# Feed-forward rows of the last quarter stored from V's buffer instead of the Q/K buffer, and one Wo load of segment 0 issued behind a flush

## The chip, the cores and the metric

The kernel runs on one core of a Trainium2 chip. The metric is device time in microseconds (us), the median of several executions; smaller is better. Five engines work side by side, each on its own queue of instructions, and wait for each other by semaphores: PE (matmuls and transposes), ACT, DVE, POOL and SP. SP does no arithmetic; it issues DMAs, and so do POOL and, in a few places, ACT. A wait holds up everything that stands behind it on the same queue.

## The reference

Two blocks work on the same `x` (2048 rows of 1024) and are mixed row by row with a gate. Block A is attention in segments of 32 rows: each segment sees its own rows and 8 memory rows that the segment before it left behind, so the segments run one after the other. Block B is a feed-forward block. All inputs are bf16.

```python
def _A_ref(x, mem0, Wq, Wk, Wv, Wo, seg_len):      # 32 heads of 128, M = 8, seg_len = 32
    ...
    for s in range(n_seg):                          # 64 segments
        xs = x[:, s * seg_len:(s + 1) * seg_len, :].copy()
        h = jnp.concatenate([mem, xs], axis=1)
        q = jnp.einsum('btd,dhe->bhte', h, Wq)
        k = jnp.einsum('btd,dhe->bhte', h, Wk)
        v = jnp.einsum('btd,dhe->bhte', h, Wv)
        scores = jnp.einsum('bhqe,bhke->bhqk', q, k) * scale
        scores = jnp.where(mask[None, None], scores, -1000000000.0)
        p = _softmax(scores, axis=-1)
        o = jnp.einsum('bhqk,bhke->bhqe', p, v)
        o = jnp.einsum('bhte,hed->btd', o, Wo)
        mem = o[:, :M, :].copy()
        outs.append(o[:, M:, :])
    return jnp.concatenate(outs, axis=1)

def _B_ref(x, w_gate, w_up, w_down):                # 3584 hidden columns
    return _gelu(x @ w_gate) * (x @ w_up) @ w_down

g = _sigmoid((x * gate_w).sum(-1, keepdims=True))
return g * a + (1 - g) * b
```

## The kernel before

**The order of the work.** First the feed-forward block runs over four quarters of 512 rows. Its results, already multiplied by 1 - g, go to `b_scr` in device memory. Then the 64 segments of block A run one by one; each adds its rows of `b_scr` at its end and stores 32 output rows. There is no planner: the order of instructions in the program text is the order on each engine's queue. A small scheduler (`_Sched`) keeps, for each named key such as `("qk", 0)`, who wrote it and who reads it. An instruction that writes a key waits for all earlier readers and writers of it, an instruction that reads a key for its writers. A DMA counts as a reader until it has landed.

**Where the weights are.** Wq, Wk, Wv and Wo don't fit on the chip beside the rest. Some of their 128-row pieces stay in `arena` for the whole run. The others are streamed in every segment through `ring`, ten places of 1024 columns, filled two at a time from a packed copy `w_scr` (line 624, on SP's queue). A load for the ring is issued when PE has read the piece that held the places.

**The end of the feed-forward block.** The last quarter is finished by `down_out` (line 499), called twice. It takes four results of 128 rows out of PSUM into four buffers: ACT takes the left halves (line 510), DVE the right halves (line 514). Each buffer is then stored to `b_scr` in five pieces (line 519). The list `bout` names the buffers and their keys: entries 0 and 1 are ring places, entry 2 is the buffer `qk`, entry 3 the buffer `oe`; `last_bout` holds two more, and the last quarter uses these two and entries 2 and 3. The pieces of entries 2 and 3 are issued on ACT's queue behind all others, those of the other buffers on POOL's. The DMA of an entry reads the entry's keys, so whoever writes the buffer next waits for its landing.

**Segment 0.** It is written out by hand (lines 1194 to 1273), as it does more than the others: it also computes q, k and v for the memory rows of the first four segments (`emit_ext`, line 862) and sets some streamed weight pieces aside (`keep`: PE transposes on line 931, a copy by DVE on line 937). The names used below:

- `emit_P` (line 980): the projections q, k, v from the rows `hT`; when a q or k projection is done, ACT copies it to `rows` (line 986).
- `emit_T`: transposes `rows` on PE (line 1019) and copies the result to `qk`, on DVE (line 1027) or on ACT (line 1025). `emit_T(0)` in segment 0 is the first writer of `qk` after the feed-forward block.
- `end_ext` (line 880) copies a finished projection of memory rows to a staging piece of the arena's chunk 20. For q and k it queues a pair (`go`, `put`): transposes on PE (line 894), four copies by DVE (line 907) and a store to `qk_scr` on POOL (line 910). `flush()` and `first_go()` issue what is queued.
- For v the staging piece is stored to `v_scr` on POOL (line 883), and `load_vte` (line 727) takes the memory rows of V from it into `vt`.
- `emit_vt` (line 1011): ACT copies V from PSUM to `vt`.
- `load_o3(k, xs)` (line 921): a load on POOL of 256 KB of Wo into quarter `k` of chunk 20, the same memory that holds the staging pieces `xs`, so it waits until those have been read. Segment 0 has four of them. Quarter 2 lies over the staging of v of the first half of the heads, quarter 1 over that of k.
- `emit_S`, `emit_PT`, `emit_PV`: scores with softmax, transposes of the probabilities, and the product with V.
- `emit_O` (line 1142): the output projection. Its last round in segment 0, `emit_O(3, ALL)`, takes the Wo pieces in the order 3, 4, 5, 6, 7, 2, 0, 1; pieces 0 to 3 are the quarters of chunk 20.

The last lines of `POOL`'s queue in segment 0 come in this order: the loads of `vt`, the store of `v_scr`, `load_o3(0, ..)`, `load_o3(2, ..)`, the store of `qk_scr` that `flush()` issues, `load_ext` (line 718), `load_x` (line 412), `load_o3(1, ..)`, a second store of `v_scr`, `load_xe` (line 418) and `load_b` (line 744).

Of the kernel before, what the change touches and what calls it, by code (L numbers as in the profile page):

```python
# [26 lines left out]
class _Sched:  # L27
# [10 lines left out]
    def op(self, eng, mk, r=(), w=(), dsem=None):  # L38
        o = _Op(eng, mk, dsem)
        deps = []  # L40
        if eng == "pool" and dsem is None:
            w = [*w, ("pool",)]
        for k in r:
            deps += self.w.get(k, ())
            if k[0] == "P":
                deps += [x for x in self.r.get(k, ()) if x.eng != eng]
        for k in w:
            deps += self.w.get(k, ())
            deps += self.r.get(k, ())
        for k in r:  # L50
            self.r.setdefault(k, []).append(o)
        for k in w:
            self.w[k] = [o]
            self.r[k] = []
        seen = set()
        for d in deps:
            if d is o or id(d) in seen:
                continue
            seen.add(id(d))
            if d.eng == eng and d.dsem is None and (eng == "pe" or eng == "sp"):  # L60
                continue
            o.deps.append(d)
            d.sig = True
        self.ops.append(o)
        return o
# [63 lines left out]
def bass_gated_mix__memory_aug_recurrent_mem_tr__geglu_ffn__prompt_kernel(  # L129
# [38 lines left out]
    with ExitStack() as es:  # L168
# [14 lines left out]
        def SB(shape, dt, name):  # L183
            return es.enter_context(nc.sbuf_tensor(name, list(shape), dt))
# [6 lines left out]
        qk = SB([128, 2, 4, L, 4], BF16, "qk")  # L191
        qkst = SB([128, 2, 4, EXT * 4], BF16, "qkst")
        vt = SB([128, 2, 512], BF16, "vt")
# [25 lines left out]
        def P(i):  # L219
            return ("P", i)  # L220
# [15 lines left out]
        def chunk(c):  # L236
            return arena[:, c * (CH // 2):min((c + 1) * (CH // 2), 21 * (CH // 2) + 2048)]
# [197 lines left out]
        def emit_H(b, j):  # L435
# [31 lines left out]
            if j % 4 == 3:  # L467
# [1 line left out]
                next_slab()  # L469

        bout = [(ring[:, RING - 2 + i, :], [("ring", RING - 2 + i, hf) for hf in range(2)]) for i in range(2)]
        bout += [(qk[:, :, :, :, :].rearrange("p a b c d -> p (a b c d)")[:, 0:1024], [("qk", 0), ("qk", 1), ("qke",)]),
                 (oe[:, :, :].rearrange("p a b -> p (a b)"), [("oe", x) for x in range(NO)])]

        last_bout = [(extra[:, :], [A(23)]), (arena[:, 21 * (CH // 2) + 1024:21 * (CH // 2) + 2048], [A(22)])]
# [111 lines left out]
        def uses(s, m, h, k):  # L587
            if m == "o":
                return 0 if k < 4 or (m, h, k) in single else (1 if (h, k) == (3, 5) else 2 * (k % 2))
            if m == "q" and h == 0 and s == 0 and k in (4, 5):  # L590
                return k - 3
            return 2 if k >= 6 and not (s and (m, h, k) == ("k", 0, 6)) else 0
# [36 lines left out]
        def slot_free(k):  # L629
            free[0] += k  # L630
            while n_str[0] < len(stream) and free[0] >= 2:
                free[0] -= 2
                stream_next()
# [78 lines left out]
        def acc(s, use):  # L712
            return (7 * s + USES[use]) % 2
# [41 lines left out]
        def unit(s, m, o, k):  # L755
            h = o // 2
            if m == "o":
                if (m, o, k) in single:
                    ap, key = single[(m, o, k)]
                    return [ap[:, 0:512], ap[:, 512:1024]], [key]  # L760
                if k >= 4:
                    sl = slot_of[(s, (m, 3, 5), 0)] if (o, k) == (3, 5) else slot_of[(s, (m, o, k - k % 2), k % 2)]
                else:
                    c, x = place[("o", o)], k
                    if o == 3:
                        y = k * 1024
                        return [chunk(c)[:, y:y + 512], chunk(c)[:, y + 512:y + 1024]], [("A20", k)]
            else:
                j = o % 2
                if (m, o, k) in single:  # L770
                    ap, key = single[(m, o, k)]
                    return [ap[:, 0:512], ap[:, 512:1024]], [key]
                if (m, h, k, j) in BACK:
                    if s > 0:
                        return BACK[(m, h, k, j)]
                    sl = slot_of[(s, (m, h, k), j if k >= 5 else 0)]
                elif k >= 6:
                    sl = slot_of[(s, (m, h, k), j)]
                elif m == "v":
                    c, x = place[("v", k)], o  # L780
                else:
                    c, x = place[(m, h, k // 2)], (k % 2) * 2 + j
            if uses(s, m, o if m == "o" else h, k) or (m == "o" and k >= 4):
                return [ring[:, sl, 0:512], ring[:, sl, 512:1024]], [("ring", sl, 0), ("ring", sl, 1)]
            return [chunk(c)[:, x * 1024 + 512 * y:x * 1024 + 512 * (y + 1)] for y in range(2)], [A(c)]
# [22 lines left out]
        def resident(m, h, kc):  # L808
            return not uses(1, m, h, kc) and not any((m, h, kc, j) in BACK for j in range(2))
# [7 lines left out]
        for s in range(NSEG):  # L817
# [20 lines left out]
            def begin(y):  # L838
                while y in order and order[0] != y:
                    later.pop(0)()  # L840
# [4 lines left out]
            def flush():  # L845
                while post:
                    go, put = post.pop(0)
                    put(go())
# [71 lines left out]
            def load_o3(k, xs):  # L920
                op("pool", lambda e: e.dma_start(chunk(20)[:, k * 1024:(k + 1) * 1024], A_Wo[24 + k, :, :]),
                   w=[("A20", k)] + [("rx", x) for x in xs], dsem=("b1", "b2", "b3", "a20")[k])
# [48 lines left out]
            def emit_P(m, h, pos, s=s):  # L971
                bank = acc(s, (m, h))
                for x in pos:
                    kc = KORD[(m, h)][x] if s else KCS.get((m, h), KCS[0])[x]
                    us = [unit(s, m, 2 * h + j, kc) for j in range(2)]

                    def mk(e, us=us, kc=kc, x=x):
                        ins = None
                        for gq in range(4):
                            ins = e.matmul(PB[bank][32 * gq:32 * gq + 32, :], lhsT=hT[:, kc, :],  # L980
                                           rhs=us[gq // 2][0][gq % 2],
                                           start=(x == 0), stop=(x == KC - 1), skip_group_check=True)
                        return ins
                    op("pe", mk, r=[("hT",)] + us[0][1] + us[1][1], w=[P(bank)])
                    if pos[-1] == KC - 1 and x == KC - 1 and m != "v":
                        op("act", lambda e: e.activation(rows[:, :], PB[bank][:, :], ACTF.Copy), r=[P(bank)], w=[("rows",)])  # L986
                    for _ in range(1 + len(kept) % 2):
                        if kept and (m, h) != ("q", 0):
                            kept.pop(0)()
                    if (m, h) in jobs and not (order and resident(m, h, kc)):  # L990
                        begin((m, h))
                        lag.append((us, kc))
                    elif (m, h) not in jobs or s:
                        slot_free(uses(s, m, h, kc))
                    if s or (m, h) == ("q", 0) or x >= 4:
                        while lag:
                            us, kc = lag.pop(0)
                            emit_ext(m, h, us + [kc])
                            held = [j for j in range(2) if s == 0 and (m, h, kc, j) in KEPT]
                            for j in held:  # L1000
                                keep(us[j], KEPT[(m, h, kc, j)], 5 if m == "q" else acc(0, ("q", 1)), 2 if j == held[-1] else 0)
                            if not held:
                                slot_free(uses(s, m, h, kc))
                    if (m, h) == ("q", 0):
                        for _ in range(1 + len(kept) % 2):
                            if kept:
                                kept.pop(0)()
# [186 lines left out]
            if s == 0:  # L1194
# [34 lines left out]
                emit_S(1)  # L1229
                emit_qke(1, ms=(0,))  # L1230
                load_o3(0, (0, 1))
                load_o3(2, (4,))
                emit_T(0, "act")
                emit_P("k", 1, (4, 5, 6, 7))
                emit_P("v", 1, (0, 1, 2))
                emit_T(1)
                emit_P("v", 1, (3,))
                flush()
                emit_P("v", 1, (4,))
                emit_PV(0)  # L1240
                emit_PT(1)
# [242 lines left out]
```

## Time and profile before

Three executions took 2459.4, 2468.72 and 2475.57 us. The profiled one took 2465.32 us.

| | before |
|---|---|
| median of the runs | 2468.72 us (2459.4 to 2475.57) |
| profiled execution | 2465.32 us |
| its span, first to last instruction | 2463.5 us |
| PE, DVE, ACT, POOL busy, share of the span | 90%, 47%, 39%, 26% |
| mean granted PE clock | 0.987 |
| moved by DMA | 781.03 MB, mean 317 GB/s |
| last quarter's feed-forward results leave PSUM | 597.9 to 600.7 us |
| segment 0 ends, segment 1 begins | about 655 us |

The profile is one execution. Each instruction has a start and a length; an engine's idle time before an instruction is put down to the semaphore that came last. Three things help in reading it. A wait can have several causes at once, and only the last one is named, so that the time that one cause costs is counted from the moment when all the others are over. The granted clock of PE is 1.00 or lower; at 0.50 matmuls take twice as long. And DMA share is the mean busy share of the core's 16 DMA engines: at 1.00 no more can be moved at a time.

### The profile page before, as it was taken

The numbers are of one execution on the slowest core, as the hardware profiler recorded it, in microseconds if no ns is written. First come the engines' busy times: TensorE is split into PE (matmuls) and PEld (weight loads), VectorE is DVE, ScalarE is ACT, GpSimd is POOL, SyncE is SP. The second block draws the span as 40 slices with busy tenths as digits, with TensorE's granted clock in tenths as the row PEclk, the third lists the DMA queues.
The fourth block names the chain that finished last, engine by engine and source line by source line (L and its number), as shares of the span: only waits on it lengthen the run. The fifth ranks groups of instructions, "written<-read, shape, count | busy, mean of one in ns | idle before, by whom it ended". The sixth has DMA issues, their size and how long they took to land.

```text
span 2463.5 us, 84811 instructions
## 1 busy us (share of the span) xinstructions
PE 2215.3 (90%) x37643; PEld 1117.8 (45%) x37699; DVE 1152.6 (47%) x3259; ACT 959.0 (39%) x2275; POOL 628.7 (26%) x1122
## 2 busy tenths in 40 slices
PE   8999999999888888988888888888888888988887
PEld 4444444444444444444444444444444444444444
DVE  5626264350444444454544444444444444444444
ACT  4314132230344444444444444444444444444443
POOL 1010102200323233232323332323323232323322
PEclk9999999999899999999999999999999999999989
DMA  8726354467899999999999999999999999999998
GB/s 263 273 69 236 118 181 128 120 214 286 304 343 363 358 363 339 363 374 358 373 368 363 363 367 364 368 370 367 359 356 361 369 371 362 371 365 361 377 372 302
DMA packets 294014, 781.03 MB, mean 317 GB/s; under 512 B 48305, under 2 KB 112993, under 8 KB 292881
## 3 DMA queue, kind: packets, MB, share of 16 engines
q1 hardware_dynamic: 240308, 703.76, 78.0%
q0 software_dynamic: 43072, 54.77, 7.3%
q10 hardware_dynamic: 10268, 17.08, 1.9%
q8 instruction: 297, 4.87, 0.8%
q14 instruction: 69, 0.56, 0.1%
HBM read 748.00 MB, written 37.22 MB: 319 GB/s over the span
## 4 chain that ended last, share of the span: by engine, by line
PE 59%; DMA 31%; DVE 5%; ACT 4%; issue 2%; POOL 0%; ACTq 0%; DVEq 0%; POOLq 0%
DMA ring<-w_scr 27%; PE pba L980 9%; PE pbb L980 9%; PE pbc L862 4%; PE pbe L1019 3%; ACT rows L986 2%; PE pba L449 2%; PE pbb L1142 2%; PE pbb L449 2%; PE pbg L449 2%; PE pbd L449 2%; PE pbf L449 2%; PE pbh L449 2%; PE pbc L449 2%; PE pbe L449 2%
## 5 line engine op out<-in xcount | busy, mean ns | idle before, releaser
L980 PE MATMUL pba<-arena,hT 128*32 128x512 bf16 x4416 | 370.9, 382 | 0.9 <-issue 0.9
L980 PE MATMUL pbb<-arena,hT 128*32 128x512 bf16 x4416 | 365.6, 383 | 0.1
L730 POOL DMA_DIRECT2D vt<-v_scr x252 | 147.1, 585 | 532.1 <-PE pbe L1100 210.2
L1094 DVE COPY ptb<-pbe 80x320 bf16<-80x320 bf16 x256 | 82.1, 321 | 317.3 <-PE pbe L1089 317.3
L862 PE MATMUL pbc<-arena,xe 128*32 128x512 bf16 x2208 | 203.9, 384 | 2.0 <-issue 1.4
L1027 DVE COPY qk<-pbe 128x512 bf16<-128x512 bf16 x129 | 89.1, 690 | 220.3 <-PE pbe L1019 211.3
L1072 ACT ACTIVATE pbd<-pbd 104x160 f32<-104x160 f32 x256 | 71.9, 281 | 299.2 <-DVE pbd L1070 299.2
L1438 POOL DMA_DIRECT2D out_dram<-bo x252 | 125.5, 505 | 201.2 <-DVE bo L1432 191.9
L980 PE MATMUL pbb<-ring,hT 128*32 128x512 bf16 x1412 | 136.4, 385 | 26.4 <-DMA ring<-w_scr 19.8
L980 PE MATMUL pba<-ring,hT 128*32 128x512 bf16 x1414 | 136.2, 383 | 26.4 <-DMA ring<-w_scr 21.3
L980 PEld LDWEIGHTS pba<-arena,hT 128*32 128x32 bf16 x4416 | 114.6, 97 | 82.2 <-issue 5.4
L980 PEld LDWEIGHTS pbb<-arena,hT 128*32 128x32 bf16 x4416 | 114.4, 97 | 79.6 <-issue 3.9
L986 ACT ACTIVATE rows<-pba 128x512 bf16<-128x512 f32 x128 | 76.4, 597 | 185.3 <-PE pba L980 183.3
L1079 DVE TENSOR_TENSOR pn<-pbd,rr 104x256 bf16<-104x256 f32 (+1 forms) x512 | 141.9, 318 | 8.7
L1142 PE MATMUL pbb<-ring,oT 128*32 128x256 bf16 x1792 | 103.7, 280 | 36.2 <-DMA ring<-w_scr 34.8
L1108 ACT ACTIVATE oT<-pbe 128x256 bf16<-128x256 f32 x256 | 97.2, 380 | 99.4 <-PE pbe L1100 97.9
L986 ACT ACTIVATE rows<-pbb 128x512 bf16<-128x512 f32 x128 | 76.4, 597 | 144.1 <-PE pbb L980 140.0
L1089 PE MATMUL pbe<-ident,pn 104*80 104x104 bf16 x1024 | 96.7, 217 | 37.3 <-DVE pn L1079 21.3
L1142 PE MATMUL pba<-ring,oT 128*32 128x256 bf16 x1792 | 102.9, 284 | 27.5 <-DMA ring<-w_scr 27.1
L1019 PE MATMUL pbe<-ident,rows 128*32 128x128 bf16 x4096 | 103.9, 221 | 26.2 <-ACT rows L986 12.5
L910 POOL DMA_DIRECT2D qk_scr<-rowsx x60 | 47.0, 783 | 308.2 <-DVE rowsx L907 306.2
L1073 DVE TENSOR_REDUCE rs<-pbd 104x4 f32<-104x160 f32 x256 | 83.0, 324 | 88.9 <-ACT pbd L1072 88.9
(268 smaller groups left out, 4529.9 us busy)
## 6 DMA issues: line engine op xcount, KB each, us to landing
ring<-w_scr SPq DMA_DIRECT2D x1153, 512.0 KB, 6.4
arena<-in_B_w_gate_dram SPq DMA_DIRECT2D x27, 1024.0 KB, 5.4
arena<-in_B_w_up_dram SPq DMA_DIRECT2D x27, 1024.0 KB, 7.6
qk<-in_A_Wq_dram ACTq DMA_DIRECT2D x63, 256.0 KB, 6.9
qkst<-qk_scr POOLq DMA_DIRECT2D x126, 64.0 KB, 5.4
qk_scr<-rowsx POOLq DMA_DIRECT2D x60, 128.0 KB, 5.6
arena<-in_B_w_down_dram SPq DMA_DIRECT2D x7, 1024.0 KB, 11.9
arena<-in_A_Wk_dram SPq DMA_DIRECT2D x6, 1024.0 KB, 6.5
```

The costliest lines, as they stand in the source:

```text
L449: ins = e.matmul(PB[bank][:, :], lhsT=wv[:, kc, col:col + 128], rhs=xb[:, kc, :], start=(kc == 0), stop=(kc == KC - 1))
L730: op("pool", lambda e: e.dma_start(vt[2 * SEG:KEYS, par, :], v_scr[s // GR, h, 2 * par:2 * par + 2, s % GR, :, :]), r=[("vscr", s // GR, h ...
L862: ins = e.matmul(PB[B_X][32 * gq:32 * gq + 32, :], lhsT=xe[:, us[-1], :], rhs=us[gq // 2][0][gq % 2], start=(n == 0), stop=(n == KC - 1), ...
L980: ins = e.matmul(PB[bank][32 * gq:32 * gq + 32, :], lhsT=hT[:, kc, :], rhs=us[gq // 2][0][gq % 2], start=(x == 0), stop=(x == KC - 1), ski ...
L986: op("act", lambda e: e.activation(rows[:, :], PB[bank][:, :], ACTF.Copy), r=[P(bank)], w=[("rows",)])
L1019: ins = e.transpose(PBV[B_T][j:j + 32, i * 128:(i + 1) * 128], rows[:, i * 128 + j:i * 128 + j + 32], ident[:, :])
L1027: op("dve", lambda e: e.tensor_copy(qk[:, m, :, 0:SEG, :], src), r=[P(B_T)], w=[("qk", m)])
L1079: op("dve", lambda e, c0=c0, k0=k0, n=n: e.tensor_tensor(out=pn[0:104, :, c0:c0 + 2 * n].rearrange("p i (two c) -> p i two c", two=2), in0 ...
L1089: ins = e.transpose(PBV[B_PT][0:KEYS, i * 128:i * 128 + 104], pn[0:104, i, :], ident[0:104, 0:104])
L1108: op("act", lambda e: e.activation(dst, src[:, :, :, 0:SEG], ACTF.Copy), r=[P(B_PV)], w=[("oT", o % 2)])
L1142: ins = e.matmul(PB[B_O][32 * q:32 * q + 32, 0:256], lhsT=oT[:, o % 2, k, :], rhs=u[q // 2][:, (q % 2) * 256:(q % 2 + 1) * 256], start=(o ...
L1438: op("sp" if last else "pool", lambda e, d=d, b=b: e.dma_start(d, b), r=[("bo", x)], w=[("out", s, x)], dsem="%s%d" % ("end" if last else ...
```

## The change

Two edits. In `bout`, entry 2 becomes the buffer `vt`, seen as 1024 columns, with the six keys `("vt", z)`, `("vte", z)` and `("vte", z, 0)`, in place of the first 1024 columns of `qk` with its three keys. Eviction, stores and queues stay as they are. In segment 0, `load_o3(2, (4,))` moves from behind `load_o3(0, (0, 1))` to behind `flush()`.

```diff
         bout = [(ring[:, RING - 2 + i, :], [("ring", RING - 2 + i, hf) for hf in range(2)]) for i in range(2)]
-        bout += [(qk[:, :, :, :, :].rearrange("p a b c d -> p (a b c d)")[:, 0:1024], [("qk", 0), ("qk", 1), ("qke",)]),
+        bout += [(vt[:, :, :].rearrange("p a b -> p (a b)"), [("vt", z) for z in range(2)] + [("vte", z) for z in range(2)] + [("vte", z, 0) for z in range(2)]),
                  (oe[:, :, :].rearrange("p a b -> p (a b)"), [("oe", x) for x in range(NO)])]
...
                 load_o3(0, (0, 1))
-                load_o3(2, (4,))
                 emit_T(0, "act")
                 emit_P("k", 1, (4, 5, 6, 7))
                 emit_P("v", 1, (0, 1, 2))
                 emit_T(1)
                 emit_P("v", 1, (3,))
                 flush()
+                load_o3(2, (4,))
                 emit_P("v", 1, (4,))
```

## The prediction

> **What bounds the kernel now.** I read the page's chain first, then the list of waits between 600 and 700 us, then the timelines around the two edited places, then the windows. By the chain, PE holds 59% of the span and DMA 31%, 27% of it ring<-w_scr. Two windows give the frame (columns of the windows: stretch, its length, busy us of PE, PEld, DVE, ACT and POOL, granted PE clock, DMA share, GB/s):
>
> ```profile
> 612.00:664.00 52.00, 41.59 (x796) 21.88 (x800) 20.22 (x67) 16.41 (x37) 15.39 (x27) 0.84 0.79 271
> 655.00:2463.00 1808.00, 1582.36 (x34076) 822.33 (x34068) 855.95 (x2790) 772.23 (x1866) 539.59 (x955) 0.99 0.99 361
> ```
>
> Three stages: feed-forward to about 600 us, segment 0 to about 655, then 63 segments of (2463.5 - 655) / 63 = 28.7 us, in which the DMA engines are full (0.99) and PE waits for the ring of weights. The diff touches only the seam between the first two stages and segment 0, where the DMA share is 0.79 and the clock 0.84: there time can go, and what goes there moves the whole tail forward unchanged. The waits there:
>
> ```profile
> DVE qk L1027 <- DMA b_scr<-qk: 9.0, 1, 9.0
> ...
> PE pbf L931 <- DVE arena L937: 4.9, 1, 4.9
> ```
>
> DVE waits 9.0 us for the store that reads qk, PE only 4.9 us behind DVE. Which of the two counts is read from the timeline (start, length, instruction, idle time before it and its releaser):
>
> ```profile
> 608.24 0.40 PE L1019 MATMUL pbe<-ident,rows 128*32 128x128 bf16 x16
> ...
> 608.78 0.62 PE L931 MATMUL pba<-ident,ring 128*128 128x128 bf16 x8
> ...
> 609.56 0.39 PE L980 MATMUL pbb<-ring,hT 128*32 128x512 bf16 x4
> 613.49 0.69 DVE L1027 COPY qk<-pbe 128x512 bf16<-128x512 bf16 x1 [8.97 <-DMA b_scr<-qk]
> 614.10 0.68 DVE L937 COPY arena<-pba 128x1024 bf16<-128x1024 bf16 x1
> 614.84 0.39 PE L931 MATMUL pbf<-ident,arena 128*128 128x128 bf16 x2 [4.89 <-DVE arena L937]
> ```
>
> The copy's own input, the transposes of line 1019, is complete at 608.24 + 0.40 = 608.64. Of DVE's 8.97 us only 613.49 - 608.64 = 4.85 are owed to the store.
>
> The second place is POOL's queue at the end of segment 0, and the PE instruction that waits at its end:
>
> ```profile
> 634.91 0.56 POOL L921 DMA_DIRECT2D arena<-in_A_Wo_dram  x1 [2.57 <-DVE qk L1027]
> 637.76 0.56 POOL L921 DMA_DIRECT2D arena<-in_A_Wo_dram  x1 [2.29 <-DMA v_scr<-arena]
> 638.39 0.76 POOL L910 DMA_DIRECT2D qk_scr<-arena  x1
> ...
> 644.09 0.54 POOL L921 DMA_DIRECT2D arena<-in_A_Wo_dram  x1 [3.60 <-DMA qk_scr<-arena]
> ...
> 649.62 0.65 PE L1142 MATMUL pba<-arena,oT 128*32 128x256 bf16 x8
> 652.05 0.41 PE L1142 MATMUL pba<-arena,oT 128*32 128x256 bf16 x4 [1.79 <-DMA arena<-in_A_Wo_dram]
> ```
>
> The second of these lines 921 is the load that is moved. It waits for the landing of v_scr's store (issued at 631.78, landed at 637.15), and the store of line 910 stands behind it on the queue; the third line 921 waits for that store's landing (643.80), lands at 644.09 + 7.92 = 652.01, and PE starts at 652.05.
>
> **The buffer, term A.** Nothing is added: the same evictions (lines 510 and 514, 0.7 us each) and the same five stores on ACT's queue, from vt. Without the wait the copy of line 1027 runs 608.69 to 609.38, the copy of line 937 follows its transposes (608.78 + 0.62 = 609.40) from 609.41 to 610.10, and PE starts line 931 at 610.15, not 614.84: 4.7 us. PE's last work before it ends at 609.95, so the gap shrinks from 4.89 to 0.2.
>
> The wait goes to V's first writers: ACT's copies of line 1011, seen at 629.0, and POOL's four loads of line 727, at 629.7. Moved forward by A and B they come at about 622.8, and the stores land at about 613.4, so the wait costs nothing with 9 us to spare. If that cover were gone, ACT would hold the softmax exponentials behind it and POOL the v_scr store. What is late next is the ring: v's second ring place is needed at 623.47 - 6.2 = 617.2. Its load is issued when the second group of line 931 frees a slot (616.80, so now about 611.4). The five ring loads from 616.80 to 626.17 took 3.7 to 6.5 us, those of 601 to 604, behind Wo and the stores, 9.1 to 9.7. The older transfers end by 612.2 (the DMA share falls to 0.17 in 612 to 613), so I take about 5 us and no wait; the other end, 9.7 us, is a wait of 3.9.
>
> **The clock, term B.** The stall throttles PE:
>
> ```profile
> 618.00:619.00 1.00, 1.00 (x13) 0.53 (x14) 0.00 (x0) 0.35 (x1) 0.00 (x0) 0.50 1.04 229
> ...
> 620.00:622.00 2.00, 2.00 (x68) 1.20 (x64) 1.06 (x5) 0.00 (x0) 0.38 (x1) 1.00 0.51 209
> ```
>
> The granted clock is 0.94 in 612 to 613, when PE has stood for 2 to 3 us, 0.50 until 619, and 1.00 from 620. From 614.84 to 619.4 PE works at clock 0.50. The eight transposes take 1.03 us there against 0.62 at 608.78, and four ext matmuls 0.62 against 0.40. Laid out at full speed, with the round trip over DVE kept (second group done at 611.32, DVE copy to 612.05, third group from 612.10, four matmuls), the ring matmuls seen at 618.99 start at 612.87, 6.12 us earlier; the transposes of line 894, which wait for ACT, come at 613.75, not 620.00. A and B together are 6.2, so B is 1.5. Its ends are 0, if a throttled window falls there all the same, and 2.2, the work halved.
>
> The Trainium skill ("TensorE: Matmul & The Clock Gate", Part 1) says that a free-running window of about 3.4 us decides, and that an idle one halves the clock. By that rule a gap of 0.2 us keeps the clock, the trace agrees for the 4.89 us gap, and A and B stand; read as a bound on single gaps it fails in the trace, where the clock is 0.50 at 650 after no PE gap over 2.0 us.
>
> **The Wo load, term C.** One POOL issue (0.56 us) moves behind flush(), past flush's store of line 910 on POOL; nothing of it crosses SP's queue. The store's data is there when DVE ends line 907 at 636.16. POOL is idle from 635.47, starts its DMAs 0.3 to 0.7 us after a release here, and issues at about 636.7, not 638.39. It lands after the same 5.41 us at 642.1, the last Wo load goes at 642.4, lands after 7.92 us at 650.3, and PE starts then instead of 652.05: 1.7 us. PE could take it from about 650.05, so at most 2.0. The loads of line 412, 418, 744 and 883 behind it come no later. The moved load, now at about 637.5 behind the store, lands after its 5.71 us at 643.2 for a use after 649: six us of cover; the slowest POOL transfer there (8.1 us) still fits. The last Wo load now shares DMA with the ring load of 640.39 that PE waits for at 646.45. Its 256 KB at the 361 GB/s of the tail are 0.7 us, so the cost is 0 to 0.7; I take 0, because it is issued 2 us after it. If the clock window of 647 to 657 (0.50) ends one step sooner, up to 1.7 us more are won; I take 0, since the 2.0 us ring wait that opens it stays.
>
> **Sum.** 4.7 + 1.5 + 1.7 = 7.9 us from span 2463.5: 2455.6. The profiled execution took 2465.32, 1.8 more than its span, so 2457.4. It lies 3.4 below the median of the runs shown, 2468.72; from that the forecast is 2461. The DMA engines can carry it: 612 to 664 moved 52 x 271 = 14.1 MB, 39 us at the tail's 361 GB/s, so 13 us are free.
>
> **Rivals.**
> *The ring is late.* The store traffic meets the earlier PE, v's second place comes at the 9.7 us of the loads of 601 to 604, PE waits 3.9, and the clock halves again for 1.5: 2.5 us gained, 2466. For it: DMA is at 0.99 to 1.05 until 612. Against: 5 us of empty DMA follow.
> *The bytes decide.* From 600 on, 64 x 285 and then 1799 us at 361 GB/s make 668 MB in 1863.5 us, 358 GB/s. If that is all the memory gives, nothing is won: 2469. Against: 397 GB/s in 608 to 610 and 375 in 850 to 900. The Trainium skill ("DMA: Bandwidth & Descriptors", Specifications) gives about 358 GB/s per core as the memory's limit, which is this rival exactly; the two windows above it speak against a hard limit.
> *The diff does more.* If DVE's whole 8.97 us were the store's, and the clock window at 647 closed, 4.1 + 1.7 more: 2455. The 608.64 above excludes the first half.
> *Slower.* In the tail a ring load that comes too late leaves PE idle, and a stretch at clock 0.50 follows, as from 804.0 to 807.4: 3.4 us at half speed, 1.7 us of PE. The three windows with clock 0.97 (800 to 850, 900 to 1000, 2000 to 2463) lose 0.03 x 613 = 18 us to them, some eleven such stretches. Where they fall depends on how loads and matmuls are phased, and the shift changes the phase. Five more outweigh 7.9 us; ten more give 2468.7 - 7.9 + 17 = 2478. For it: the three runs of one kernel span 16 us. Against: no edit touches a segment after the first, so such events are as likely to be fewer. For over 1%, twenty more are needed.
>
> **Chances.** Forecast 0.62, ring late 0.13, bytes 0.08, more 0.07, slower 0.10. About 1% (24.7 us) is what a measurement of this kernel tells from no change, the runs shown spreading 0.65%. All cases but extreme ones of the last two lie inside it: faster 0.04, same 0.93, slower 0.03. The range: the forecast's own terms run from 7.9 - 1.5 - 0.7 to 7.9 + 0.7 + 0.3 + 1.7, so 2458 to 2463; taking in the late ring and the bytes (2469) and half the 16 us spread of the runs at the lower end gives 2450 to 2470.
>
> **What would show it.** Right: DVE's line 1027 starts near 608.7 with a releaser on PE; no PE gap over 1 us before line 931 and the clock at 1.00 from 600 to 635; line 910 ahead of the second line 921 on POOL, about 5.4 us before the last Wo load; PE's last line 1142 at about 644; segment 1 some 8 us sooner. Wrong: a PE wait on ring<-w_scr near 617, ACT's line 1011 released by b_scr<-vt, or a tail longer than 1808 us.

## The result, and the profile after

The changed kernel takes 2456.09 us (median of 18 runs, 2448.88 to 2471.76), the kernel before, in the same sessions, 2465.99 us (18 runs, 2456.58 to 2475.57). The ratio is 0.9965, with a 95% interval of 0.9948 to 0.9982: 4.4 to 12.8 us less. The forecast was 7.9 us less.

The profiled execution has a span of 2447.1 us, 16.4 below the one of before. That is more than the medians say, and the marks of the two traces show where it comes from. From here on "the seam" is the time from the first eviction of the last quarter (ACT, line 510) to the transposes of line 1420 that end segment 0, and "the tail" what follows.

| | before | after | difference |
|---|---|---|---|
| start to first eviction | 597.93 | 595.79 | -2.14 |
| seam | 55.01 | 47.84 | -7.17 |
| tail | 1810.56 | 1803.44 | -7.12 |
| span | 2463.5 | 2447.1 | -16.4 |

Only the seam holds an edit; the other two rows come back below. The timeline of the changed kernel around the first edit (start, length, instruction, idle time before it and its releaser):

```profile
606.15 0.40 PE L1019 MATMUL pbe<-ident,rows 128*32 128x128 bf16 x16
606.37 0.39 PE L980 MATMUL pbb<-arena,hT 128*32 128x512 bf16 x4
606.60 0.69 DVE L1027 COPY qk<-pbe 128x512 bf16<-128x512 bf16 x1 [4.21 <-PE pbe L1019]
606.70 0.62 PE L931 MATMUL pba<-ident,ring 128*128 128x128 bf16 x8
607.25 0.40 PE L862 MATMUL pbc<-arena,xe 128*32 128x512 bf16 x4
607.35 0.69 DVE L937 COPY arena<-pba 128x1024 bf16<-128x1024 bf16 x1
607.47 0.39 PE L980 MATMUL pbb<-ring,hT 128*32 128x512 bf16 x4
608.10 0.56 PE L931 MATMUL pbf<-ident,arena 128*128 128x128 bf16 x7 [0.24 <-DVE arena L937]
```

DVE still sits idle for 4.21 us before its copy, now until PE's transposes are done: this part of the 8.97 us was never the store's. PE waits 0.24 us in place of 4.89. Windows (stretch, length, busy us of PE, PEld, DVE, ACT and POOL, granted clock, DMA share, GB/s) show the clock at 1.00 through the place where it fell to 0.50, and the DMA engines without the hole that stood there. The first line is from the kernel before, behind its stall, the other two from the changed kernel:

```profile
614.80:617.00 2.20, 2.16 (x20) 1.76 (x24) 0.24 (x1) 0.00 (x0) 0.00 (x0) 0.50 0.04 7
```

```profile
600.00:612.00 12.00, 11.04 (x204) 6.07 (x200) 3.47 (x6) 2.28 (x4) 2.70 (x5) 1.00 1.01 349
612.00:620.00 8.00, 7.52 (x178) 4.03 (x174) 5.42 (x23) 1.48 (x4) 3.16 (x5) 1.00 0.91 337
```

POOL's queue at the end of segment 0, changed kernel:

```profile
623.15 0.56 POOL L883 DMA_DIRECT2D v_scr<-arena  x1
626.24 0.56 POOL L921 DMA_DIRECT2D arena<-in_A_Wo_dram  x1 [2.52 <-DVE qk L1027]
627.98 0.76 POOL L910 DMA_DIRECT2D qk_scr<-arena  x1 [1.18 <-DVE arena L907]
628.98 0.54 POOL L921 DMA_DIRECT2D arena<-in_A_Wo_dram  x1 [0.24 <-issue]
...
635.50 0.54 POOL L921 DMA_DIRECT2D arena<-in_A_Wo_dram  x1 [3.64 <-DMA qk_scr<-arena]
```

The store of line 910 now goes ahead of the moved load. But the last Wo load comes 7.52 us after it, against 644.09 - 638.39 = 5.70 before. The view of the store alone gives its time from issue to landing, min, median and max, first before, then after:

```profile
DMA to landing us min/median/max: 5.4/5.4/5.4
```

```profile
DMA to landing us min/median/max: 7.2/7.2/7.2
```

In these two profiles the 1.8 us by which the store is issued sooner are lost before it lands. What still waits at the end of the seam, on PE, changed kernel:

```profile
637.56 0.61 PE L1142 MATMUL pba<-ring,oT 128*32 128x256 bf16 x8 [1.51 <-DMA ring<-w_scr]
...
642.74 0.40 PE L1142 MATMUL pba<-arena,oT 128*32 128x256 bf16 x4 [0.98 <-DMA arena<-in_A_Wo_dram]
```

### The profile page after: what moved, and what is told of

Read it like the earlier page. It is cut to its first block, busy times and chain, and to the rows that moved or that the text cites. A ratio compares the mean times of both kernels' runs of the same rounds, so it can differ in the third digit from the quotient of the medians.

```text
span 2447.1 us, 84869 instructions
## 1 busy us (share of the span) xinstructions
PE 2212.5 (90%) x37699; PEld 1115.9 (46%) x37699; DVE 1153.2 (47%) x3259; ACT 958.3 (39%) x2275; POOL 628.5 (26%) x1122
## 4 chain that ended last, share of the span: by engine, by line
PE 60%; DMA 30%; DVE 4%; ACT 4%; issue 2%; POOL 0%; SPq 0%; DVEq 0%; POOLq 0%
DMA ring<-w_scr 28%; PE pba L980 9%; PE pbb L980 9%; PE pbc L862 4%; PE pbe L1019 3%; ACT rows L986 3%; PE pbb L1142 2%; PE pba L449 2%; PE pbb L449 2%; PE pbd L449 2%; PE pbe L449 2%; PE pbg L449 2%; PE pbf L449 2%; PE pbh L449 2%; PE pbc L449 2%; PE pbe L1089 2%
```

## The experiments

The two theories to tell apart: that the seam is shortened by the buffer and the clock (6.2 us) and the load (1.7), as predicted; or that the load's part is taken back by other transfers, so that only the first 6 us are won. Marks are counted from the first eviction of line 510, as the feed-forward block before it ended between 595.6 and 597.9 us in the profiles.

**The buffer edit alone**

```diff
-        bout += [(qk[:, :, :, :, :].rearrange("p a b c d -> p (a b c d)")[:, 0:1024], [("qk", 0), ("qk", 1), ("qke",)]),
+        bout += [(vt[:, :, :].rearrange("p a b -> p (a b)"), [("vt", z) for z in range(2)] + [("vte", z) for z in range(2)] + [("vte", z, 0) for z in range(2)]),
```

> Only the buffer edit; the Wo load stays where it was. Measure: the seam, from the first eviction of line 510 to the transposes of line 1420 that end segment 0. It is 55.0 us in the kernel before and 47.8 in the changed one. My steps (store wait 4.7, clock 1.5) give 55.0 - 6.2 = 48.8, and a total 6.2 us below the kernel before (ratio 0.9975). A rival says that the whole 8.97 us idle time of DVE was the store's: then the seam is about 46. A second rival says that the shift is lost again at the ring: seam over 52.

Measured: 2456.61 us (median of 12) against 2464.23, ratio 0.9973 (0.9952 to 0.9994), so 6.7 us less. DVE's copy of line 1027 comes 10.76 us after the first eviction; in the kernels with the old buffer it was 15.12 to 15.56. The transposes of line 894 come at 15.54; with the old buffer at 21.51 to 22.07 (the run below with added matmuls left aside). The seam is 48.31. The rival with the whole 8.97 us would need 46, the one with the loss at the ring over 52. Both fall. This run also bears on the load, which is not moved here: the store of v_scr ahead of it landed after 3.85 us (5.37 in the kernel before), so the store of line 910 was issued 16.86 us after line 894, almost as early as with the load moved. It took 7.50 us and landed 24.37 after line 894; in the kernel before it landed 23.80 after it.

**The Wo load alone**

```diff
                 load_o3(0, (0, 1))
-                load_o3(2, (4,))
...
                 flush()
+                load_o3(2, (4,))
```

> Only the Wo load of quarter 2 behind the flush; the buffer stays qk. My step C: the store of line 910 goes 1.7 us sooner, keeps its 5.4 us to landing, and the seam falls from 55.0 to 53.3. The rival, from the changed kernel's trace, where that store took 7.2 us: the store goes sooner into the same queue of transfers, behind two ring loads of 512 KB, and lands when they are through; then it takes about 7 us, the last Wo load is issued no sooner against line 1142, and the seam falls by 0 to 0.7. In the total both are too small to be told from no change (ratio 0.9993 or 1.0).

Measured: 2460.5 us (median of 12) against 2464.23, ratio 0.9992 (0.9969 to 1.0015), no difference that can be told. The seam is 53.47, which alone would be the 53.3 of step C. But the kernel before, profiled once more (below), gives 53.42 with no edit at all, so this mark decides nothing. The store took 6.00 us to land instead of 5.41, between the two theories. It landed 22.60 us after line 894, in the two profiles of the kernel before 23.80 and 23.50 after it: some 1 us of the 1.8 is left here. Inconclusive by itself.

**The clock alone**

```diff
                     op("pe", mk, r=[("hT",)] + us[0][1] + us[1][1], w=[P(bank)])
+                    if s == 0 and (m, h, x) == ("k", 0, 6):
+                        def spin(e):
+                            ins = None
+                            for _ in range(22):
+                                ins = e.matmul(PB[7][:, :], lhsT=ident[:, :], rhs=chunk(0)[:, 0:512], start=True, stop=True)
+                            return ins
+                        op("pe", spin, r=[("ident",), A(0)], w=[P(7)])
```

> The kernel before, its store wait kept, with 22 matmuls of 128x512 (0.215 us each, 4.7 us) into a free PSUM bank where PE stands for 4.89 us; they compute nothing that is used. If the stall's second price is the clock (term B), the granted clock stays 1.00, DVE's copy of line 1027 comes as late as before, and from line 931 on PE is 1.5 to 1.9 us sooner: the seam falls from 55.0 to 53.1 to 53.5. If the clock costs nothing there (other waits would fill the time), the seam stays 55.0.

The timeline of this kernel, where the added lines move line 1027 to 1034; L989 are the 22 matmuls:

```profile
608.41 4.92 PE L989 MATMUL pbh<-arena,ident 128*128 128x512 bf16 x22
611.76 0.69 DVE L1034 COPY qk<-pbe 128x512 bf16<-128x512 bf16 x1 [8.71 <-DMA b_scr<-qk]
612.36 0.68 DVE L937 COPY arena<-pba 128x1024 bf16<-128x1024 bf16 x1
613.17 0.61 PE L931 MATMUL pbf<-ident,arena 128*128 128x128 bf16 x8
```

and its windows:

```profile
608.50:613.50 5.00, 5.00 (x28) 2.38 (x28) 1.29 (x2) 0.00 (x0) 0.00 (x0) 1.00 0.45 157
613.50:618.00 4.50, 4.26 (x89) 2.48 (x90) 1.75 (x6) 1.19 (x2) 0.00 (x0) 1.00 0.56 186
```

The wait for the store is all there (8.71 us, the copy at 15.31), yet the clock stays at 1.00 and the eight transposes of line 931 take 0.61 us, not 1.03. Line 894 comes 19.98 us after the first eviction. With the old buffer and no such matmuls it comes at 22.07, 21.51 and 21.77 in three profiles, 21.78 on average: the clock is worth 1.8 us, 1.5 to 2.1 against the single profiles. Its seam of 52.92 is 1.3 below the mean of the two profiles of the kernel before, 54.2; the one run took 2458.96 us.

**The kernel before once more**

> The kernel before once more, for what two profiles of one kernel differ by. If the marks of the seam are fixed, the seam is 55.0 again to 0.3 us and the store of line 910 behind the v_scr store lands after 5.4 us again, while the tail (line 1420 of segment 0 to the end) may differ from 1810.6 us by up to 8 us, as the 16 us spread of the runs has to come from somewhere. If the seam differs by over 1 us, the terms of the seam can't be read from single profiles.

Measured (one run, 2466.78 us): first eviction at 595.64 us, line 894 at 21.51, the seam 53.42, the tail 1815.83, the store's landing 5.15. So the 2.14 us of the first row of the table, too, come with no edit at all. The seam differs by 1.6 us between two profiles of one kernel, more than the 0.3 that I had set for fixed marks. Step C, of that size, can't be read from one seam; the early marks, which repeat to 0.6, can.

**The ring loads held back**

```diff
+            hold = [("qkscr", 0, 1, 1)] if s == 0 and u in (("o", 1, 6), ("o", 2, 4)) else []
             op("sp", lambda e: e.dma_start(ring[:, sl:sl + wd, :].rearrange("p a b -> p (a b)"), src),
-               r=[("rp", u)], w=[("ring", y, x) for y in slots for x in range(2)], dsem=f"ring{sl}")
+               r=[("rp", u)] + hold, w=[("ring", y, x) for y in slots for x in range(2)], dsem=f"ring{sl}")
```

> The changed kernel, with the two ring loads (512 KB each) that stand just ahead of the store of line 910 held back until that store has landed. My present theory of the lost part of step C is that the store lands when the ring loads ahead of it are through. Then without them it lands 4 to 5.5 us after its issue instead of 7.2, and the last Wo load goes some 2 us sooner; PE pays for it, as it must wait for the ring at line 1142, and the seam grows from 47.8 to over 50. Rival: the store takes 7 us because of what POOL queues behind it (the moved Wo load) or of itself; then it stays at 6.5 to 7.5.

The store alone in this kernel:

```profile
DMA to landing us min/median/max: 3.8/3.8/3.8
```

It lands after 3.8 us, even sooner than expected, and the last Wo load goes at 37.25 us after the first eviction instead of 39.70. PE no longer waits for it, but for the ring:

```profile
636.19 0.40 PE L1143 MATMUL pba<-ring,oT 128*32 128x256 bf16 x8 [2.16 <-DMA ring<-w_scr]
639.99 0.61 PE L1143 MATMUL pba<-ring,oT 128*32 128x256 bf16 x8 [1.20 <-DMA ring<-w_scr]
```

The seam is 48.83, longer than the 47.84 of the changed kernel by 1 us, less than expected and within what a seam repeats to; the one run took 2452.6 us. One thing more differs: v_scr's store landed late here, so the moved Wo load was issued 3.3 us behind the store of line 910, and not 1.0. By itself this run does not tell the ring loads from the moved load; the next one, with the ring loads in front and the moved load 3.9 us behind, does, and its store took 6.18 us. Together they put most of the store's time down to the ring loads ahead of it. The other profiles say the same: in all nine with those loads in front, the store lands between 0.65 us before and 1.12 us after the second of them. In the kernel before, the ring load landed at 643.14 and the store at 643.80; in the changed one at 635.39 and 635.21. The store's own time, by contrast, runs from 5.15 to 7.56 us.

**The moved load further back**

```diff
                 flush()
-                load_o3(2, (4,))
...
                 load_x(1)
+                load_o3(2, (4,))
                 load_o3(1, (2, 3))
```

> The changed kernel, with the Wo load of quarter 2 moved further back on POOL, behind load_x. If that load's 256 KB, issued 1 us behind the store of line 910, are what slows the store, the store lands 5.4 us after its issue again and the seam falls from 47.8 by up to 1.5. If the ring loads ahead of it do, the store keeps 6.5 to 7.5 us, and the seam stays at 47.8 or grows, as the load of quarter 2 now comes about 3 us later.

Measured: the store lands after 6.18 us, between the two expectations (7.24 and 6.91 in the two profiles of the changed kernel), 0.65 us before the second ring load (636.17). The seam is 46.97, the shortest of all, 0.9 below that of the changed kernel and within the 1.6 us by which a seam fails to repeat. The run doesn't exclude that the moved load has a small part in the delay. The one run took 2469.13 us, with a tail of 1823.16.

**A place of its own for k's second half**

```diff
             if x == 5:
                 return rowsx[:, :], RX, "rowsx"
+            if x == 3:
+                return oe[:, 16:32, :].rearrange("p a b -> p (a b)"), [("oe", 2), ("oe", 3)], "rx3"
...
+                load_o3(1, (2,))
                 load_o3(0, (0, 1))
...
                 load_x(1)
-                load_o3(1, (2, 3))
```

> The changed kernel, with the staging of k's second half in a free half of oe, so that the last Wo load (quarter 1) needn't wait for its store: it is issued ahead of load_o3(0). This removes the wait at the end of segment 0 altogether, of which step C was to remove 1.7. PE waits 0.98 us for that load in the changed kernel's profile; without it the seam falls from 47.8 to 46.5 to 47.0, and the total by 1 us, which can't be told from no change. Rival: the transfers that the earlier load pushes back make the ring load that line 1142 waits for as much later, and the seam stays at 47.8.

PE at the end of this kernel's seam (line 1142 is 1144 here):

```profile
638.52 0.62 PE L1144 MATMUL pba<-ring,oT 128*32 128x256 bf16 x8 [2.20 <-DMA ring<-w_scr]
...
642.08 0.86 PE L1144 MATMUL pba<-arena,oT 128*32 128x256 bf16 x12
```

The wait for Wo is gone, the last round runs through, and the wait for the ring is 2.20 us where it was 1.51 (1.35 in the second profile of the changed kernel). The seam is 47.67, 0.2 less. In total 2454.08 us (median of 12) against 2461.71, ratio 0.9962 (0.9944 to 0.9979), which is not apart from the 0.9965 of the changed kernel. The longer wait for the ring is what the rival says, and the DMA engines are nearly full in the last 15 us of the seam (share 0.96 in 628 to 643, in this kernel as in the changed one), so that what one transfer wins another may lose. A seam that repeats to 1.6 us can't tell 47.8 from the expected 46.5 to 47.0, so the rival is likely and not shown.

**The changed kernel once more**

> The changed kernel once more. By the two profiles of the kernel before, the seam repeats to about 1.6 us and the mark of line 894 to 0.6: here 47.8 +- 1.6 and 15.6 +- 0.6. The tail should not repeat the 1803.4 us of the first profile: in four profiles of kernels whose tail is the same program it ran from 1807.8 to 1815.8, so I expect 1803 to 1816, the longer the more time at clock 0.50 it holds. If the tail is 1803 again, the change does something to the tail.

Measured (one run, 2457.38 us): line 894 at 15.54, the seam 48.33, the tail 1809.79, span 2455.6. The 1803.4 of the first profile doesn't repeat. Over the ten profiles the tail follows the time that it holds at clock 0.50:

| kernel | at clock 0.50 in the tail, us | tail, us |
|---|---|---|
| changed | 31.9 | 1803.4 |
| ring loads held back | 37.7 | 1805.8 |
| clock alone | 39.7 | 1807.8 |
| load alone | 44.9 | 1813.0 |
| changed, again | 48.5 | 1809.8 |
| before | 49.3 | 1810.6 |
| buffer alone | 50.3 | 1811.6 |
| own place | 53.8 | 1815.1 |
| before, again | 68.2 | 1815.8 |
| load further back | 75.5 | 1823.2 |

A straight line through them is 1792 us plus 0.40 us for each us at clock 0.50 (correlation 0.94). It doesn't say which of the two causes the other, as a wait of PE makes the tail longer and can lower the clock as well, as the 4.89 us one did. The two profiles of one kernel differ by 6.4 and by 5.3 us. So the tail's 7.12 us in the first table are not shown to belong to the change.

## Why the prediction was right, and where it was off

**Term A, the wait: right.** The copy comes 10.76 to 10.81 us after the first eviction in all six profiles with vt, against 15.12 to 15.56 in the four with qk: 4.6 us on average, forecast 4.8 (613.49 to 608.69) at the copy and 4.7 at PE. Counting from the end of the copy's own input, and not the 8.97 us of the list of waits, was the step that mattered, and the buffer alone confirmed it.

**Term B, the clock: right.** Forecast 1.5, measured 1.8 with the wait kept, and 1.5 to 2.1 by single profiles. A and B together were forecast at 6.2 us at line 894; they measured 21.78 - 15.54 = 6.2.

**Where the waits went: right.** ACT's copies of line 1011 run at 620.38, straight behind a copy (line 880) that PE released, some ten us after the stores from vt landed. The ring load for v's second place was issued at 609.24, 13.45 us after the first eviction (forecast 13.5), and landed after 4.26 us (forecast about 5), 1.35 us before its use. The rival of the late ring didn't occur.

**Term C, the Wo load: the step that failed in its size.** The prediction had the store of line 910 land "after the same 5.41 us". Its issue was forecast well: 1.7 us sooner, measured 1.8 against line 894 (16.60 us after it instead of 18.39). But a landing time taken from one place was carried to another, 1.8 us closer behind two ring loads of 512 KB each, and the store lands about when the second of these does. With the load moved it lands 22.6 to 24.2 us after line 894 (five profiles with the ring loads in front), with the load in its old place 23.5 to 24.5 (four): 0.7 us sooner on average, not 1.7. The wait that C was to take away, PE's for the last Wo load, was 1.79 and 1.34 us in the two profiles of the kernel before, and 0.98 and 2.30 in those of the changed kernel. In the seam C is worth 0.2 us (buffer alone 48.31, both edits 48.09 on average) to 0.8 (load alone 53.47, before 54.2 on average), both below what a seam repeats to. The prediction weighed this contention for the last Wo load's effect on the ring, at 0 to 0.7 us, and not for the store.

**The sum.** Over the profiles the seam fell from 54.2 to 48.1 us, 6.1 in place of 7.9; the medians fell by 9.9, with an interval of 4.4 to 12.8 that holds both. The 3.8 us by which the medians fell further than the seam are not accounted for; with tails that differ by up to 20 us between profiles, nothing shows that they belong to the change. That the total fell by as much as forecast, and more, with C mostly missing, is in part luck. The forecast of 2461 us also started from the median of three runs, 2468.72, where 18 runs give 2465.99. And the prediction held that only about 1% can be told from no change: with 18 runs of each kernel, 0.35% could.

**The rivals.** The one in which the bytes decide, with nothing won, lies outside the interval. Of the figure that the Trainium skill gives in "DMA: Bandwidth & Descriptors" (Specifications), some 358 GB/s per core, this case shows no hard limit: the tail averages 363 GB/s in the changed kernel. The slower rival has its mechanism in the traces, as the table of tails shows, but no sign that the change drives it. The 1.7 us that the forecast left open for the second clock window weren't won: the clock is at 0.50 from 637.1 for 10.2 us in the changed kernel, as from 647.0 before.

**Not settled.** How much of the store's delay the moved load itself makes (the run with that load further back lies between the theories), whether C is worth anything in the total, and why the tails differ in their time at clock 0.50.

## What to carry to other kernels

When a wait has several causes, count from the moment the second last is over: here 4.85 of 8.97 us. A stall of PE that is long enough to lower its clock costs more than its length, here 4.9 us and another 1.8, and filling it with idle matmuls shows how much. And a DMA that is issued sooner behind larger ones need not land sooner: before counting on it, look at what landed just before it, and whether its own landing moves with that.

## What the runs showed of the hardware that was not expected

A small store on POOL's queue landed about when the second of two large loads did that were issued before it on SP's queue: 128 KB took 3.8 us in the one run without them just ahead and 5.2 to 7.6 us behind them, in nine profiles. The Trainium skill ("DMA: Bandwidth & Descriptors", Issuing engines are not separate DMA queues) says that transfers of all issuing engines run on the same DMA engines and interleave; the traces fit that, and show that interleaving did not let the small one through much sooner: it landed between 0.65 us before and 1.12 us after the second load.

The clock also fell where no single gap of PE was long. From 643.0 to 646.4 in the kernel before, PE was busy for 1.06 of 3.4 us in pieces, its longest gap 2.0 us, and the clock was at 0.50 from 647.0:

```profile
643.00:646.40 3.40, 1.06 (x25) 0.55 (x24) 1.22 (x5) 1.25 (x4) 2.12 (x4) 1.00 0.99 360
...
646.45 0.40 PE L1142 MATMUL pba<-ring,oT 128*32 128x256 bf16 x8 [1.99 <-DMA ring<-w_scr]
```
